# Linear attention and a mixture of four experts on one core: five weight sums change engine, the first batch's small copies are merged, and the start is put in another order

## The chip, the core and the metric

The kernel runs on one core of a Trainium2 chip. The time is device time of one execution in microseconds; a comparison is made between medians of several executions. All times of single instructions below come from one execution that the hardware profiler recorded. The engines are called as in the profile: PE (TensorE), PEld (its weight loads), DVE (VectorE), ACT (ScalarE), POOL (GpSimd) and SP (SyncE, which here only issues DMAs).

## The reference

Two stages follow each other. With `phi(x) = where(x > 0, x, exp(x) - 1) + 1`:

```python
q_p, k_p = phi(q), phi(k)                          # 8 batches, 8 heads, 576 tokens, 64 wide
kv  = einsum('bhsd,bhse->bhde', k_p, v)             # 64 x 64 for each head
z   = sum(k_p, axis=s)
x   = einsum(q_p, kv) / (einsum(q_p, z) + 1e-06)   # 4608 tokens x 512
p   = probs / (probs.sum(-1) + 1e-09)
out = sum over e of p[:, e] * (relu(x @ w1[e]) @ w2[e])   # w1: 512 x 1024, w2: 1024 x 512, 4 experts
```

The kernel computes `phi(x)` as `min(exp(x), max(x + 1, 1))`: one exponential on ACT, one linear part (add, then max) on DVE or POOL, and one minimum on DVE.

## The kernel before, in words

**Tiles.** The 4608 tokens are nine tiles of 512: the first 512 tokens of each of the eight batches, and one tile of all that is left over. A tile passes through the attention of its batch and then through all four experts. Both layers of an expert are done as seven products of quarter blocks in place of eight (a scheme of Strassen's kind). `Block` (L841 to L941) is layer 1, with the products p1, p2, p6, p5, p7, p4, p3 and the sum c22; `layer2_product` (L806) is layer 2, called m in the lists (m12.51 is the fifth product for tile 1, expert 2). The scheme needs sums of weights: `weight_sums` (L758, the steps s0.0 to s3.3, DVE) for w1 and `weight_sums2` (L775, the steps t0.0 to t3.3) for w2. Step t2.1 is part 1 of expert 2. Each is one subtraction of 128x1024 fp16 elements with both inputs in SBUF. Sums of hidden values (L797 to L803, hs) and of tokens (L868, ts) run on POOL. Tile 0 does layer 1 of expert 0 without the scheme, in `layer1_half` (L675, steps L00 to L31, each cut into pieces), and layer 2 of its experts as plain matmuls (y). The sums of w2 are therefore read from tile 1 on alone.

**Batch 0.** Batch 0 has code of its own, the class `First`. Its inputs come in pieces: k and v by pairs of heads (`load_kv`, lk0 to lk3 and lv0 to lv3), q in four pieces of 128x512 (`load_q`, lq0 to lq3). For each piece of k there is an exponential (`k_exp`, L583, ke), a linear part (`k_lin`, L586, kl) and a minimum (`k_min`, L590, km); v is cast (`v_cast`, L593, vc, on the engines of `VC`: pieces 0 and 3 POOL, 1 DVE, 2 ACT). For q the same three are qe (L601), ql (L604) and qm (L607), and then a transposition of four blocks on PE with a copy (`q_turn`, L615, qT). `kv` (L621 to L639) makes kv and z of a pair of heads: 18 matmuls of 64x65 into one PSUM tile, the two heads on different partitions, and then two copies of 64x65 into `kvz`, whose other blocks hold zeros from a memset (L199). `CFG["KC"]` says which engine does each of the eight copies. `x_norm` (L648 to L652, steps nd00 to nd11) multiplies q by `kvz` and normalises; `x_half` (L662, xT) transposes x, after which layer 1 of tile 0 can start. The step nd01 needs pairs 0 and 1, nd11 and nd10 pairs 2 and 3.

**What sets the order.** Every step is a Python generator. The order on every engine is that in which the steps are advanced. For the start of the kernel, up to tile 1, it is the list `CFG["EARLY"]`: a name in it advances that step by one piece, so that a name which stands twice first issues its matmuls and later its copy. What the list does not name is sorted by due positions behind it. The list orders DMAs as well: steps w100 to w231 are 512 KB loads of weights (w1 of expert 1, first half, is w110; w2 of expert 1 is w210 and w211), issued by POOL, and k0 to v3, q0 to q3, rk and rv are later batches' loads on POOL. The first loads of batch 0 are issued by SP and ACT. `warm` (L1016) puts matmuls on PE that only read zeros (`qz`) and compute nothing; `CFG["WARM"]` says how many go with each warm step.

**Engines at the change.** In `QL`, the i-th letter says where the linear part of q's piece i runs: V is DVE, P is POOL. In the list before, the first steps of q are in the order qe0, ql0, ql3, qm0, and pieces 2 and 3 follow behind piece 0's.

Of the kernel before, what the change touches and what calls it, by code (L numbers as in the profile page):

```python
# [11 lines left out]
FP32 = mybir.dt.float32  # L12
FP16 = mybir.dt.float16
AO = mybir.AluOpType
# [22 lines left out]
            kv=34.0,  # L37
# [19 lines left out]
            kv=19.1,  # L57
# [15 lines left out]
            kv=19.1,  # L73
# [21 lines left out]
    "QL": 'VVPV',  # L95
    "QT": 'AAAA',
    "KC": ('AA', 'AV', 'VA', 'AA'),
# [3 lines left out]
    "WARM": (14, 3, 2, 1, 5),  # L101
    "BANK": {'qT0': 'py', 'qT1': 'b', 'nd00': 'py', 'nd00+': 'b', 'kv2': 'py', 'xT00': 'b', 'kv3': 'b', 'nd10+': 'b', 'L00': 'b', 'L10': 'py', 'nd01': 'b', 'xT01': 'py', 'nd11+': 'b', 'L20': 'e', 'L30': 'e', 'L01': 'e', 'L11': 'py', 'L21': 'py', 'L31': 'b', 'b1.qT3': 'py', 'b1.nd30': 'py', 'b1.nd21': 'b', 'b1.q1': 'b', 'b1.qT1': 'py', 'b1.nd01': 'py', 'b1.xT2': 'b', 'b1.nd11': 'py', 'b1.xT0': 'b'},
    "EARLY": (
# [36 lines left out]
def kernel(  # L140
# [10 lines left out]
    nc = tc.nc  # L151
# [6 lines left out]
    P = 128  # L158
    HP = P // 2
# [37 lines left out]
    for i in range(2):  # L197
        kvz = pconst.tile([P, NPAIR, 2, DE], FP16, tag=f"kvz{i}", name=f"kvz{i}")
        nc.vector.memset(kvz, 0.0)  # L199
        kvzs.append(kvz)  # L200
# [26 lines left out]
    def aps(shape, dtype, name, more=""):  # L227
        return ppm.tile(shape, dtype, tag=CFG["BANK"].get(now[0] + more, "s"), bufs=2, name=name)
# [321 lines left out]
    class First(Batch):  # L550
# [70 lines left out]
        def kv(self, i, engs):  # L621
            ps = aps([P, DE], FP32, "psum_kv")
            for t in range(TK):
                for u in range(2):
                    us = slice(u * HP, (u + 1) * HP)
                    nc.tensor.matmul(
                        out=ps[us],
                        lhsT=kpos[us, i, t],
                        rhs=vpos[us, i, t],
                        start=t == 0,  # L630
                        stop=t == TK - 1,
                        skip_group_check=True,
                    )
            for u in range(2):
                yield
                us = slice(u * HP, (u + 1) * HP)
                (engs[u].copy if engs[u] is nc.scalar else engs[u].tensor_copy)(
                    out=self.kvz[us, i, u], in_=ps[us]
                )  # L639
# [135 lines left out]
    def weight_sums2(e, part):  # L775
        if part == 0:
            t2_sb[e] = pw.tile([P, 3, FH, DH], FP16, tag=f"t2_{e}", name=f"t2_{e}")
        w, tw = w2_sb[e], t2_sb[e]
        b11, b12 = w[:, 0:FH, 0:DH], w[:, 0:FH, DH:Dm]
        b21, b22 = w[:, FH:FC, 0:DH], w[:, FH:FC, DH:Dm]  # L780
        if part == 0:
            nc.vector.tensor_tensor(out=tw[:, 0], in0=b12, in1=b11, op=AO.subtract)
        elif part == 1:
            nc.vector.tensor_tensor(out=tw[:, 1], in0=b22, in1=tw[:, 0], op=AO.subtract)
        elif part == 2:
            nc.vector.tensor_tensor(out=tw[:, 2], in0=b21, in1=tw[:, 1], op=AO.subtract)
        else:
            nc.vector.tensor_tensor(out=b12, in0=b22, in1=b12, op=AO.subtract)
# [234 lines left out]
    with tc.manual_schedule(  # L1023
# [7 lines left out]
        def put_at(pos, name, *g):  # L1031
            work.append((pos, len(work), name, g))

        put_at(0, "lpr0", load_probs, nc.sync, True)
        for i in range(4):
# [11 lines left out]
            put_at(0, f"kv{i}", b0.kv, i, [on[y] for y in CFG["KC"][i]])  # L1047
# [122 lines left out]
```

## Time and profile before

| | us |
|---|---|
| median of 3 runs (484.61 to 485.6) | 484.77 |
| the profiled execution | 484.06 |
| its span | 482.3 |
| PE busy | 474.5 |
| DVE, ACT, POOL busy | 377.6, 331.4, 356.1 |
| first real matmul of layer 1 (L675) | 16.10 |
| weights landed: w110, w111, w200, w201 | 20.74, 23.28, 26.39, 29.34 |
| w120, w121, w130, w131 | 33.41, 35.90, 48.30, 51.65 |
| w220, w221, w231, w230 | 55.68, 58.80, 61.31, 63.97 |

The span is that of the profiled execution; 1.8 us of its time lie around it. A row of the timeline has the start, the duration, the engine, the line, the operation with its output and inputs, and the size; "x2" joins neighbouring rows of one line, and the brackets name the idle time ahead and the instruction that ended it. A row of the windows gives the busy time of every engine in a stretch; the number before the last but one is the granted clock of PE, and the next the DMA engines' mean busy share (it can exceed 1).

### The profile page before, as it was taken

How to read it: one execution, taken by the hardware profiler on the slowest of the kernel's cores; microseconds unless marked ns; L12 is line 12 of the kernel's file. 1: busy time of each engine (PE TensorE's matmuls, PEld its weight loads, DVE VectorE, ACT ScalarE, POOL GpSimd, SP SyncE). 2: the span in 40 equal slices, each digit the busy share in tenths (PEclk: the TensorE clock that was granted, in tenths of full speed). 3: DMA queues.
4: the chain of work that ended last, by engine and by line, in shares of the span. 5: the costliest groups of instructions: out<-in, count | busy, mean ns of one | idle time of the engine just before them, and what ended most of it. 6: DMA issues, size and time to landing. Idle time of an engine off the chain costs nothing.

```text
span 482.3 us, 12013 instructions
## 1 busy us (share of the span) xinstructions
PE 474.5 (98%) x4565; PEld 407.4 (84%) x4565; DVE 377.6 (78%) x794; ACT 331.4 (69%) x662; POOL 356.1 (74%) x340
## 2 busy tenths in 40 slices
PE   7999999999999999999999999999999999999997
PEld 3766766898889888998889888988898888888886
DVE  5778988997868895889679885988787756775677
ACT  4689989956895599649874888478954465446540
POOL 5566044789866986789777977697769877987775
PEclk9999999999999999999999999999999999999999
DMA  8999986442445154533552436323230020003002
GB/s 292 219 218 256 232 212 210 124 112 83 135 140 115 39 160 154 119 59 117 173 134 62 112 123 170 78 73 112 65 68 12 2 88 2 0 1 89 2 1 87
DMA packets 80025, 53.67 MB, mean 111 GB/s; under 512 B 45088, under 2 KB 72736, under 8 KB 79968
## 3 DMA queue, kind: packets, MB, share of 16 engines
q1 hardware_dynamic: 69920, 40.56, 30.6%
q0 software_dynamic: 8800, 11.27, 12.1%
q10 hardware_dynamic: 1248, 1.08, 0.7%
q8 instruction: 35, 0.57, 0.5%
q14 instruction: 22, 0.18, 0.1%
HBM read 45.16 MB, written 9.44 MB: 113 GB/s over the span
## 4 chain that ended last, share of the span: by engine, by line
PE 96%; DVE 1%; DMA 1%; issue 0%; ACT 0%; SPq 0%; DVEq 0%
PE py L830 39%; PE pb L887 25%; PE pe L887 19%; PE py L735 6%; PE ph L675 1%; PE psum_nd L492 1%; PE psum_kv L464 1%; DMA rawq<-in_q_dram 1%; PE pb L830 1%; PE pe L830 1%; DVE kpos L586 0%; PE psum_nl L510 0%; PE psum_num L648 0%; PE psum_xh L662 0%; DVE qp L607 0%
## 5 line engine op out<-in xcount | busy, mean ns | idle before, releaser
L726 DVE SCALAR_TENSOR_TENSOR acc<-py,p_sb,acc 128x256 f32<-128x256 f32 (+1 forms) x382 | 182.3, 489 | 42.3 <-PE py L830 38.3
L871 DVE CUSTOM_DVE_ANT_0 h<-pe,u 128x512 f16<-128x512 f32 x140 | 96.2, 689 | 45.5 <-PE pe L887 27.8
L887 PEld LDWEIGHTS <-w 128*128 128x128 f16 x1120 | 108.9, 98 | 16.2
L797 POOL TENSOR_TENSOR hs<-h 128x512 f16<-128x512 f16 x64 | 74.6, 1165 | 56.9 <-DVE h L871 52.8
L830 PEld LDWEIGHTS <-h 128*128 128x128 f16 x1024 | 99.6, 98 | 11.5
L830 PE MATMUL py<-w,h 128*128 128x256 f16 x744 | 106.4, 273 | 0.0
L898 ACT COPY u<-pb 128x512 f32<-128x512 f32 x140 | 82.5, 592 | 29.9 <-PE pb L887 27.8
L799 POOL TENSOR_TENSOR hs<-hs,h 128x512 f16<-128x512 f16 x64 | 73.9, 1155 | 26.3 <-PE py L830 23.8
L887 PEld LDWEIGHTS <-s 128*128 128x128 f16 x840 | 81.2, 98 | 12.0 <-DVE s L767 0.2
L887 PE MATMUL pb<-tt,w 128*128 128x256 f16 x560 | 83.9, 273 | 0.0
L830 PEld LDWEIGHTS <-hs 128*128 128x128 f16 x768 | 74.5, 98 | 8.8 <-issue 0.2
L803 POOL TENSOR_TENSOR hs<-h,hs 128x512 f16<-128x512 f16 x64 | 74.4, 1162 | 0.9 <-PE py L830 0.7
L830 PE MATMUL py<-t,hs 128*128 128x256 f16 x496 | 74.1, 273 | 0.0
L801 POOL TENSOR_TENSOR h<-h 128x512 f16<-128x512 f16 x64 | 73.9, 1154 | 0.1
L920 ACT ACTIVATE h<-pe 128x512 f16<-128x512 f32 x70 | 42.0, 601 | 41.3 <-PE pe L887 40.7
L913 ACT COPY pe<-pb 128x512 f32<-128x512 f32 x70 | 40.0, 572 | 42.0 <-PE pb L887 15.8
L941 ACT ACTIVATE h<-pb 128x512 f16<-128x512 f32 x70 | 41.9, 601 | 6.0 <-PE pb L887 5.9
L887 PE MATMUL pe<-tt,s 128*128 128x256 f16 x280 | 42.0, 273 | 0.0
L887 PE MATMUL pb<-tt,s 128*128 128x256 f16 x280 | 41.8, 273 | 0.0
L887 PE MATMUL pe<-xT,s 128*128 128x256 f16 x248 | 37.1, 273 | 0.0
L887 PE MATMUL pb<-xT,w 128*128 128x256 f16 x248 | 37.1, 273 | 0.0
L830 PE MATMUL py<-w,hs 128*128 128x256 f16 x248 | 37.0, 273 | 0.0
(132 smaller groups left out, 594.4 us busy)
## 6 DMA issues: line engine op xcount, KB each, us to landing
w<-in_moe_w_dram POOLq DMA_DIRECT2D x14, 512.0 KB, 10.6
out_dram<-acc SPq DMA_DIRECT2D x28, 256.0 KB, 2.6
rawb<-in_k_dram SPq DMA_DIRECT2D x24, 256.0 KB, 3.0
rawb<-in_q_dram SPq DMA_DIRECT2D x24, 256.0 KB, 2.7
rawb<-in_v_dram SPq DMA_DIRECT2D x24, 256.0 KB, 2.7
out_dram<-acc SPq DMA_DIRECT2D x12, 128.0 KB, 2.4
w<-in_moe_w_dram POOLq DMA_DIRECT2D x4, 256.0 KB, 5.5
rawb<-in_k_dram POOLq DMA_DIRECT2D x4, 256.0 KB, 10.4
```

Source lines behind the costliest of these rows:

```text
L726: nc.vector.scalar_tensor_tensor(out=acc, in0=ps, scalar=pscal, in1=acc, op0=AO.mult, op1=AO.add)
L797: nc.gpsimd.tensor_tensor(out=hs[0], in0=a21, in1=a22, op=AO.add)
L799: nc.gpsimd.tensor_tensor(out=hs[1], in0=hs[0], in1=a11, op=AO.subtract)
L801: nc.gpsimd.tensor_tensor(out=a21, in0=a11, in1=a21, op=AO.subtract)
L803: nc.gpsimd.tensor_tensor(out=hs[3], in0=a12, in1=hs[1], op=AO.subtract)
L830: nc.tensor.matmul(out=ps, lhsT=lhsT(k), rhs=rhs[:, k], start=first and k == 0, stop=k == FH - 1, skip_group_check=True,)
L871: nc.vector._custom_dve(TENSOR_ADD_SAT, out=out, in0=ps, in1=u, s0=BIG, s1=0.0)
L887: nc.tensor.matmul(out=ps[:, kk], lhsT=lk(kc), rhs=rhs[:, kc], start=first and kk == 0 and kc == 0, stop=kc == 1, skip_group_check=True,)
L898: nc.scalar.copy(u, self.b)
L913: nc.scalar.copy(self.e5, self.b)
L920: nc.scalar.activation(self.h[:, :, 0, 0:NH], self.e5, AF.Relu)
L941: nc.scalar.activation(self.h[:, :, 1, 0:NH], self.b, AF.Relu)
```

## The change

Four things are changed.

- `QL` is VVVV: the linear part of q's piece 2 (128x512) runs on DVE where POOL did it.
- `kv` of batch 0 writes the two heads of a pair into separate columns of a 128x130 PSUM tile. One matmul of zeros (128x130) opens the tile, and one copy of 128x130 on ACT, zeros and all, takes the place of the two of 64x65. The memset of the first `kvz` goes.
- `TP` names five parts of `weight_sums2` (t2.0, t2.1, t2.2, t3.0 and t3.1) that run on POOL; the others stay on DVE.
- `WARM` has 26 matmuls in place of 25, 13 at first and then single ones. `EARLY` is written anew for all engines and reaches a few steps further. In its start the pieces of q stand in the order in which they land: piece 2 and 3 ahead of piece 0. Of the first four weight loads w101 moves up; the loads behind w111 come as rk0, rk1, w200, k2, w201, k1, w120, w121, k0, w210, k3, v0, q1, w211 and so on; the last ones as w220, q3, w221, q2, w230, then t2.0 on the same engine, and w231 behind it.

```diff
-    "QL": 'VVPV',
+    "QL": 'VVVV',
     "QT": 'AAAA',
-    "KC": ('AA', 'AV', 'VA', 'AA'),
+    "TP": {2: (0, 1, 2), 3: (0, 1)},
+    "KC": 'AAAA',
...
-    "WARM": (14, 3, 2, 1, 5),
+    "WARM": (13,) + (1,) * 13,
...
     "EARLY": (
-        "lq2 lq3 lq0 lk0 qe0 ql0 ql3 qm0 kl0 lk1 lpr0 ke0 km0 qe2 ql2 qm2 lv0 ke1 kl1 km1 warm0 qT0 lv1 lk2 qe3 qm3 warm1 qT2 qT0 vc0 w100 warm2 kv0 vc1 qT2",
-        "warm3 kv1 lk3 kv0 kv0 kl2 kv1 kl3 w102 kv1 nd01 lv3 nd01 warm4 xT11 xT01 ke2 km2 qT3 w103 vc3 lv2 ke3 vc2 nd00 w101 km3 xT01 w110 xT11 w111 kv3 k3 kv2",
...
+        "lq2 lq3 warm0 lk0 lq0 qe2 qe3 lk1 ql2 ql3 qe0 qm3 ql0 qm2 qm0 kl0 ke1 ke0 km0 lpr0 lv0 lv1 warm1 warm2 warm3 warm4 warm5 qT0 warm6 lk2 qT2 vc0 lk3",
+        "w100 w102 warm7 warm8 lv3 qT2 qT0 ke2 kl1 vc1 lv2 km1 warm9 kv0 w101 w103 vc3 kv0 ke3 w110 warm10 kl3 km3 kl2 w111 rk0 rk1 w200 k2 w201 k1 w120 w121",
+        "k0 w210 k3 v0 q1 w211 lq1 rv0 v2 rv1 v3 v1 q0 w130 w131 kv1 warm11 kv1 nd01 warm12 nd01 vc2 qe1 warm13 nd00 qT3 xT01 xT11 kv3 xT01 qT3 xT11 ql1 km2",
...
-        nc.vector.memset(kvz, 0.0)
+        if i:
+            nc.vector.memset(kvz, 0.0)
...
-        def kv(self, i, engs):
-            ps = aps([P, DE], FP32, "psum_kv")
+        def kv(self, i, eng):
+            ps = aps([P, 2, DE], FP32, "psum_kv")
+            nc.tensor.matmul(
+                out=ps.rearrange("p u d -> p (u d)"),
+                lhsT=qz[:, 0, 0],
+                rhs=qz.rearrange("p a u c -> p (a u c)")[:, 0 : 2 * DE],
+                start=True,
+                stop=False,
+                skip_group_check=True,
+            )
             for t in range(TK):
                 for u in range(2):
                     us = slice(u * HP, (u + 1) * HP)
                     nc.tensor.matmul(
-                        out=ps[us],
+                        out=ps[us, u],
                         lhsT=kpos[us, i, t],
                         rhs=vpos[us, i, t],
-                        start=t == 0,
+                        start=False,
                         stop=t == TK - 1,
                         skip_group_check=True,
                     )
-            for u in range(2):
-                yield
-                us = slice(u * HP, (u + 1) * HP)
-                (engs[u].copy if engs[u] is nc.scalar else engs[u].tensor_copy)(
-                    out=self.kvz[us, i, u], in_=ps[us]
-                )
+            yield
+            (eng.copy if eng is nc.scalar else eng.tensor_copy)(out=self.kvz[:, i], in_=ps)
...
     def weight_sums2(e, part):
+        eng = nc.gpsimd if part in CFG["TP"].get(e, ()) else nc.vector
...
-            nc.vector.tensor_tensor(out=tw[:, 0], in0=b12, in1=b11, op=AO.subtract)
+            eng.tensor_tensor(out=tw[:, 0], in0=b12, in1=b11, op=AO.subtract)
...
```

The other parts of `weight_sums2` take `eng` in the same way.

More of the change, by code (lines that the diff above doesn't have):

```diff
@@ L781, in weight_sums2 @@
         if part == 0:
-            nc.vector.tensor_tensor(out=tw[:, 0], in0=b12, in1=b11, op=AO.subtract)
+            eng.tensor_tensor(out=tw[:, 0], in0=b12, in1=b11, op=AO.subtract)
         elif part == 1:
-            nc.vector.tensor_tensor(out=tw[:, 1], in0=b22, in1=tw[:, 0], op=AO.subtract)
+            eng.tensor_tensor(out=tw[:, 1], in0=b22, in1=tw[:, 0], op=AO.subtract)
         elif part == 2:
-            nc.vector.tensor_tensor(out=tw[:, 2], in0=b21, in1=tw[:, 1], op=AO.subtract)
+            eng.tensor_tensor(out=tw[:, 2], in0=b21, in1=tw[:, 1], op=AO.subtract)
         else:
-            nc.vector.tensor_tensor(out=b12, in0=b22, in1=b12, op=AO.subtract)
+            eng.tensor_tensor(out=b12, in0=b22, in1=b12, op=AO.subtract)
     def hidden_sum(h, hs, i):
@@ L1046 @@
             put_at(0, f"qT{i}", b0.q_turn, i, on[CFG["QT"][i]])
-            put_at(0, f"kv{i}", b0.kv, i, [on[y] for y in CFG["KC"][i]])
+            put_at(0, f"kv{i}", b0.kv, i, on[CFG["KC"][i]])
             put_at(0, f"nd{i // 2}{i % 2}", b0.x_norm, i // 2, i % 2)
```

58 rows, old and new, of the table nl are left out of this document.

## The prediction

> **What bounds the kernel now.** I read the busy shares first, then the chain that ended last, then the table of windows, and only then single rows of the timeline. The page says that TensorE carries the span:
>
> ```profile
> PE 474.5 (98%) x4565; PEld 407.4 (84%) x4565; DVE 377.6 (78%) x794; ACT 331.4 (69%) x662; POOL 356.1 (74%) x340
> ...
> PE 96%; DVE 1%; DMA 1%; issue 0%; ACT 0%; SPq 0%; DVEq 0%
> ```
>
> The reader is to see that an engine other than PE can matter only where PE has a hole. The windows tell where the holes are (start and end, length, then the busy time of PE, PEld, DVE, ACT and POOL with counts, the granted clock and the DMA share):
>
> ```profile
> 0.00:5.00 5.00, 3.80 (x9) 1.35 (x10) 1.53 (x4) 1.28 (x1) 1.56 (x10) 1.00 0.55 170
> 5.00:10.00 5.00, 3.61 (x25) 1.40 (x25) 3.57 (x8) 3.72 (x7) 3.50 (x4) 1.00 1.06 399
> 10.00:15.00 5.00, 3.73 (x72) 2.45 (x72) 4.24 (x11) 3.04 (x10) 4.98 (x9) 1.00 1.20 256
> 15.00:20.00 5.00, 4.67 (x88) 4.09 (x87) 3.71 (x11) 3.09 (x10) 2.91 (x5) 1.00 1.17 211
> 20.00:25.00 5.00, 5.00 (x50) 4.48 (x48) 3.91 (x9) 3.83 (x9) 1.97 (x3) 1.00 1.17 239
> ```
>
> From 20 us on PE is full, and it stays so to about 479 us. Before that most of its busy time is warm-up matmuls (L1016), which compute nothing. I counted PE's columns: the real matmuls hold 456.5 us at full rate. Of these 3.62 us lie ahead of the first step of layer 1 (L675, 16.10 us), so 12.48 us are lost there; by 22.9 us the loss is 12.60 us, and it grows by only 0.1 us up to 117 us. Some 3 us more are the tail. So the change can win only in the first 16 us, and can lose wherever it opens a hole in the full stretch behind. The DMA share is above 1.0 from 5 to 64 us: weights arrive at a fixed pace, and that is the second bound.
>
> What sets the 16.10 us is the chain of batch 0. Its middle in the timeline (start, duration, engine, line; in brackets the idle time ahead):
>
> ```profile
> 11.04 1.33 DVE L586 TENSOR_SCALAR kpos<-krawt 128x576 f16<-128x576 f32 x2
> 11.18 0.48 PE L626 MATMUL psum_kv<-vpos,kpos 64*64 64x65 f16 x18 [0.49 <-DVE vpos L593]
> ...
> 11.70 0.21 ACT L637 CAST kvz<-psum_kv 64x65 f16<-64x65 f32 x1 [0.86 <-PE psum_kv L626]
> ...
> 12.40 0.23 DVE L637 CAST kvz<-psum_kv 64x65 f16<-64x65 f32 x1
> 12.68 0.22 PE L648 MATMUL psum_num<-kvz,qT 128*128 128x128 f16 x1 [0.77 <-DVE kvz L637]
> ```
>
> The reader is to see that pair 1's sums are ready near 11.7 us, but the second half of their copy stands behind two linear parts on VectorE until 12.40, and PE waits 0.77 us for it.
>
> **Part 1: the first q pieces, VVPV to VVVV and a new order.** Ahead of that middle stand these rows:
>
> ```profile
> 4.33 1.92 POOL L604 TENSOR_SCALAR qp<-rawq 128x512 f16<-128x512 f32 x1 [2.90 <-DMA rawq<-in_q_dram]
> ...
> 6.22 0.76 DVE L604 TENSOR_SCALAR qp<-rawq 128x512 f16<-128x512 f32 x2 [3.71 <-DMA rawq<-in_q_dram]
> 6.22 0.63 ACT L601 ACTIVATE ee<-rawq 128x512 f16<-128x512 f32 x1 [3.06 <-DMA rawq<-in_q_dram]
> ```
>
> Pieces 2 and 3 landed at 4.25 and 4.61 us, but ACT and DVE queue them behind piece 0, which landed at 6.20. The order after puts them first: linear parts at 4.3 and 4.7 (0.42 us, in place of POOL's 1.92), exponentials at 4.3 and 4.8 (0.62), one minimum at 5.5 (0.42). From 6.2 only piece 0 and one minimum are left, so k's linear part starts near 7.25 and pair 0's minimum ends near 8.7. With the same row durations I get kv0 at 8.8 (before 9.89) and kv1 at 10.45 (11.18), which now waits for the second v cast. That is 0.7 us at kv1.
>
> **Part 2: one copy for a pair.** Two 64x65 copies (ACT 0.21, DVE 0.23) become one 128x130 copy on ACT; by the 64x65 row below and the 128x512 copy (0.59) above I take 0.28 us. It no longer stands behind VectorE: pair 1 is copied at about 11.43, the numerators run at 11.5 where the second half ran at 12.68, the normalisation at 12.05 instead of 13.03. PE pays one 128x130 zero matmul a pair, 4 x 0.055 = 0.22 us. The zero memset of one buffer (0.49 us) lies in the idle start of DVE and gains nothing.
>
> From there ql1, km2 and qm1 (DVE), the second normalisation (14.0 to 14.9) and the copy of xT11 follow, and I get the first layer-1 step at **14.45 us** against 16.10. Ahead of it lie 3.62 + 0.22 + 0.09 = 3.93 us of PE work, as the order of PE's steps shows, 0.22 of them the zeros. Loss: 14.45 - 3.71 = 10.74 against 12.60, that is **1.86 us won if nothing is late behind it**.
>
> **What is late next.** Two things. First, weights. Their landing times hardly move, as the first loads keep their order and the queue is full: w110 20.74, w111 23.28, w120 32.5, w131 51.6, w220 54.9, w221 58.1 (those behind w111 shifted by where the new order of POOL's issues puts each, at 2.55 us for 512 KB). Counting 0.108 us for each 256-wide matmul ahead, the first use of each lies 6.06, 8.66, 18.2, 36.64, 39.7 and 42.3 us of PE work behind the first L. A hole opens unless the first L, without holes, would start at 14.68, 14.62, 14.3, 15.0, 15.2 and 15.8. So landings alone take the start back to about 15.0 to 15.8 in effect. Second, small waits that I find by laying the new order over the row durations: nd11 for pair copies 0.15, nd10 for a q copy 0.3, first cuts of the third and fourth L group 0.2, p5.010 behind three ACT operations of batch 1 0.4, batch 1's kv 0.25. They sum to 1.3 us. A PE delayed by one of them is no longer early for the weights, so the two do not add: effective start 14.45 + 1.3 = 15.75, past all landings but the last by 0.05. Gain 1.86 - 1.3 = **0.56, say 0.6 us**.
>
> **Part 3: five sums of layer 2 to POOL.** On DVE a 128x1024 sum takes 0.69 us, 5 x 0.61 start to start = 3.0 us freed between 60 and 115 us. POOL's 128x512 sums take 1.155 us (64 of them), so 1024 take 2.2 us, an estimate, 11 us in all. Their first readers are products of tile 1 after 109 us, and POOL was idle 47 to 64 us, so the duration itself costs nothing: even 3.5 us each would move only the first hidden sums. Freed DVE time is worth nothing where PE is full (below nothing excluded; above, the 0.1 us of drift bounds it). What is not free is this:
>
> ```profile
> 64.36 1.16 POOL L868 TENSOR_TENSOR tt<-xT 128x512 f16<-128x512 f16 x1 [16.89 <-ACT xT L536]
> ...
> 67.65 1.15 POOL L868 TENSOR_TENSOR tt<-xT 128x512 f16<-128x512 f16 x1
> ```
>
> ```profile
> 65.23 0.84 DVE L788 TENSOR_TENSOR w<-w 128x1024 f16<-128x1024 f16 x1
> ...
> 68.44 0.90 DVE L782 TENSOR_TENSOR t<-w 128x1024 f16<-128x1024 f16 x1
> ```
>
> Usual is 0.69. The two sums start while POOL's sum runs and end 0.55 and 0.54 us after POOL's end: as if they got going only when POOL let go, less 0.15. [...]
>
> [...] Bounds 0 and 2.05 us; I take 0 for the forecast, as t2.0 cannot start before w220 has landed (about 55), when s3.0, s3.1 and s3.3 (52 to 53.7 now) are done, and keep the rest as a rival.
>
> WARM goes from 25 to 26 matmuls (0.43 us at first, 0.213 after 5.87 us); they fill waits in PE, and the clock was granted at 1.00 throughout. Single ones between steps may delay a step by up to 0.2 us; this is in the range. [...]
>
> **Sum.** 484.06 (profiled) - 0.6 = 483.46; the median of the runs is 0.71 above the profiled execution, so 484.77 - 0.6 = **484.2**.
>
> **Rivals.**
> - *Full head gain* (0.22). The small waits do not come or lie side by side, and the landings allow a start of 14.7 to 15.0: gain 12.60 - (14.7 to 15.0 - 3.71) = 1.6 to 1.3 us, 483.2 to 483.5. For it: the waits are read from modelled ends of matmuls. Against it: w131, w220 and w221 bind at 15.0 to 15.8.
> - *The change does not do what it says* (0.18). The chain is early but the weights, or the new waits, take all back: loss again 12.4 to 12.8, gain 0.2 to -0.2, 484.6 to 485.0. For it: w200 (slack 0.58 before) and w221 have next to none after. One landing 0.4 us later than I put it takes 0.4.
> - *Blocked sums* (0.15), the slower end. POOL's 2.2 us sums hold s3.2 or t0.2, and with them batch 1's normalisations that PE waits for. One block of 2.05 less 0.3 slack, less the gain of 0.6, is 1.15 us slower, 485.9; it decides from a block of 0.9 us on.
> - *Forecast* (0.45): 0.2 to 1.2 us faster, 483.6 to 484.6.
>
> **How the numbers follow.** 0.2% is 0.97 us, about what a measurement of this kernel can tell from no change. Faster by more: the full gain 0.22 and a third of the forecast, 0.37. Slower by more: most of the blocked sums and a few hundredths of late landings, 0.17. Within: 0.46. The range runs from the full gain with its 1.86 us, 482.9, to one block, 486.0; beyond it lie two blocks, or late landings and a block.
>
> **What would show it.** Right: kv1 near 10.5 and its single copy by 11.5; first L675 row near 14.5; then small PE holes of 0.1 to 0.4 between 15 and 60 us, summing to some 1.3 us, most released by DVE, ACT or weights' DMA; POOL rows of 2.2 us at L787 to L793. Wrong: holes of over 1 us at p6.030 or batch 1's x with a DVE row of 1.5 to 2.7 us in front (blocked); no holes and a first L at 14.5 (full gain); a first L at 16 or later, through a kv1 that still waits for v; or warm-up rows at 0.43 us after 7 us.

## The result, and the profile after

The changed kernel takes 485.75 us (median of 22 runs, 485.44 to 488.06), the kernel before 484.63 us (22 runs, 483.85 to 486.41): a ratio of 1.0026 with a 95% interval of 1.0016 to 1.0036, some 1.3 us slower (1.1 by the two medians), where 0.6 us faster was forecast. The profiled execution of the changed kernel, 486.91 us with a span of 485.1, is one of its longer ones (15 of the 22 have spans of 483.7 to 484.2); its stalls are therefore read here for their causes, and the sizes are taken from the medians and ratios of the experiments.

Page of the kernel after, the busy times and the chain that ended last:

```profile
PE 476.7 (98%) x4570; PEld 408.2 (84%) x4570; DVE 374.9 (77%) x787; ACT 332.4 (69%) x660; POOL 365.5 (75%) x344
...
PE 90%; DVE 3%; ACT 3%; DMA 1%; issue 1%; ACTq 0%
```

Six per cent of the chain have left PE (96% before): two went to DVE (1% before), three to ACT (0% before) and one to issue (0% before); DMA has kept its 1%. The windows of the kernel after (columns as before) say where:

```profile
15.00:20.00 5.00, 4.96 (x61) 4.25 (x59) 3.71 (x10) 2.36 (x8) 2.84 (x4) 1.00 1.16 208
...
25.00:30.00 5.00, 4.67 (x36) 3.34 (x35) 2.81 (x9) 4.47 (x10) 2.60 (x4) 1.00 1.18 240
...
60.00:65.00 5.00, 3.74 (x33) 2.46 (x32) 4.97 (x10) 3.40 (x7) 2.15 (x2) 1.00 0.72 129
```

The last of these stretches in the kernel before:

```profile
60.00:65.00 5.00, 5.00 (x44) 3.25 (x43) 4.89 (x11) 3.14 (x6) 0.64 (x1) 1.00 1.08 198
```

The stretch 15 to 20 is fuller than before (4.96 in place of 4.67), as meant. But PE, which had no hole from 20 us on, now has one of 1.26 us between 60 and 65 and smaller ones at 25 to 30 (0.33), 50 to 55 (0.16) and from 75 to 100 (0.44 in all). Counted by PE's columns as in the prediction, the loss is 11.24 us at the first L (before 12.48 there), 12.55 at 53 us (before 12.46), and in this execution 3 us more by 120 us, where before adds 0.3. Such a count is good to some 0.2 us: the prediction has 12.60 for before at 22.9 us, and a loss cannot shrink; and by the matmul rows that the traces hold, after is still 0.2 us ahead at 53. So the head did win, the win was gone by 53 us as nearly as this can tell, and the slowdown arises behind it.

Timeline of the kernel after, the engines around the largest hole:

```profile
57.90 2.12 POOL L792 TENSOR_TENSOR t<-w,t 128x1024 f16<-128x1024 f16 x1 [0.42 <-DMA w<-in_moe_w_dram]
57.97 2.60 DVE L776 TENSOR_TENSOR s<-w,s 128x1024 f16<-128x1024 f16 x1
60.49 0.67 DVE L375 SCALAR_TENSOR_TENSOR qp<-qp,psum_ee 128x512 f16<-128x512 f16 x1
61.63 0.74 DVE L733 SCALAR_TENSOR_TENSOR acc<-py,p_sb,acc 128x512 f32<-128x512 f32 x1
62.43 0.38 PE L451 MATMUL psum_qT<-identh,qp 128*128 128x128 f16 x4 [1.19 <-DVE acc L733]
```

VectorE's sum s3.2 (L776) starts 0.07 us behind POOL's t2.1 (L792) and takes 2.60 us where its like takes 0.69; it ends 0.55 us behind POOL's end. What stands behind it on VectorE comes some 1.9 us late, and PE stands still for a PSUM tile that the accumulation (L733) has to read first. This is the rival that I had called blocked sums.

And the timeline of the kernel after in the head:

```profile
10.82 0.90 DVE L593 TENSOR_TENSOR kpos<-kexp,kpos 128x576 f16<-128x576 f16 x1 [0.35 <-ACT kexp L586]
11.36 0.88 POOL L596 CAST vpos<-vrawt 128x576 f16<-128x576 f32 x1
11.64 0.91 DVE L589 TENSOR_SCALAR kpos<-krawt 128x576 f16<-128x576 f32 x1
12.48 0.19 DVE L658 RECIPROCAL recip<-psum_den 128x8 f32<-128x8 f32 x1
13.45 0.40 PE L669 MATMUL psum_xh<-identh,x_sb 128*128 128x128 f16 x4 [1.14 <-DVE x_sb L659]
```

Two rows of VectorE around POOL's cast take 0.90 in place of 0.45; PE waits 1.14 us for the normalisation behind them. The first L675 step (now L682) came at 15.05 us: 1.05 earlier than before, 0.6 later than I had put it.

### The profile page after: what moved, and what is told of

It is laid out like the page before. It is cut to its first block, busy times and chain, and to the rows that moved or that the text cites. A ratio compares the mean times of both kernels' runs of the same rounds, so it can differ in the third digit from the quotient of the medians.

```text
span 485.1 us, 12019 instructions
## 1 busy us (share of the span) xinstructions
PE 476.7 (98%) x4570; PEld 408.2 (84%) x4570; DVE 374.9 (77%) x787; ACT 332.4 (69%) x660; POOL 365.5 (75%) x344
## 4 chain that ended last, share of the span: by engine, by line
PE 90%; DVE 3%; ACT 3%; DMA 1%; issue 1%; ACTq 0%
PE py L838 39%; PE pb L895 23%; PE pe L895 18%; PE py L742 3%; PE warm_ps L1024 1%; PE psum_nd L495 1%; PE ph L682 1%; PE psum_kv L467 1%; DMA rawb<-in_k_dram 1%; PE pb L838 1%; DMA out_dram<-acc 1%; ACT pe L921 1%; ACT psum_ee L370 1%; PE pe L838 1%; DVE h L879 1%
## 5 line engine op out<-in xcount | busy, mean ns | idle before, releaser
L733 DVE SCALAR_TENSOR_TENSOR acc<-py,p_sb,acc 128x256 f32<-128x256 f32 (+1 forms) x382 | 182.0, 488 | 44.7 <-PE py L838 38.0
L805 POOL TENSOR_TENSOR hs<-h 128x512 f16<-128x512 f16 x64 | 74.4, 1162 | 53.1 <-DVE h L879 48.7
L807 POOL TENSOR_TENSOR hs<-hs,h 128x512 f16<-128x512 f16 x64 | 74.4, 1162 | 25.2 <-PE py L838 21.5
L838 PEld LDWEIGHTS <-hs 128*128 128x128 f16 x768 | 74.4, 98 | 8.7 <-issue 0.2
L838 PE MATMUL py<-t,hs 128*128 128x256 f16 x496 | 74.4, 273 | 0.0
L895 PE MATMUL pe<-xT,w 128*128 128x256 f16 x248 | 37.2, 273 | 0.0
```

Of the source, the lines that this page charges most:

```text
L733: nc.vector.scalar_tensor_tensor(out=acc, in0=ps, scalar=pscal, in1=acc, op0=AO.mult, op1=AO.add)
L805: nc.gpsimd.tensor_tensor(out=hs[0], in0=a21, in1=a22, op=AO.add)
L807: nc.gpsimd.tensor_tensor(out=hs[1], in0=hs[0], in1=a11, op=AO.subtract)
L838: nc.tensor.matmul(out=ps, lhsT=lhsT(k), rhs=rhs[:, k], start=first and k == 0, stop=k == FH - 1, skip_group_check=True,)
L895: nc.tensor.matmul(out=ps[:, kk], lhsT=lk(kc), rhs=rhs[:, kc], start=first and kk == 0 and kc == 0, stop=kc == 1, skip_group_check=True,)
```

## The experiments

Theory A: where a sum of VectorE and a POOL operation meet, one holds the other until it is through, as the two rows of before suggest (0.84 and 0.90 us in place of 0.69, ended 0.55 and 0.54 us behind POOL's sum); POOL's 2.1 us sums hold s3.2 or t0.2, and batch 1's normalisations behind them. Theory B: the new order of the start loses the time, wherever the sums run. All ratios are to the kernel before on the same chip.

**The sums back on VectorE, in their places.**

```diff
-    "TP": {2: (0, 1, 2), 3: (0, 1)},
+    "TP": {},
```

> The kernel after with its five sums back on VectorE, at the places the list gives them; all else as after. Theory A (POOL's sum blocks s3.2): the row of s3.2 (2.60 us at 57.97 in the trace of after) falls to about 0.7, PE's hole of 1.36 us at 62.4 goes, and the time comes to 484.3 to 484.9, that is, 0.9 to 1.4 us under after. Theory B (the new order of the start and its small waits lose the time, the engine of the sums does not matter): still 485.4 or more. Theory C (VectorE's 3.0 us of relief are worth something): slower than after, 486 or more.

Measured: 491.73 us, ratio 1.0145 (1.0127 to 1.0164). Theory A's and theory B's numbers are missed; theory C's (the relief of VectorE is worth something, 486 or more) is met, but by a wait that it did not name. The hole at 62 is gone, but the list has four of the sums side by side, and on VectorE they run into POOL's token sums. Timeline and then PE's waits of this run:

```profile
66.62 0.68 DVE L790 TENSOR_TENSOR t<-w 128x1024 f16<-128x1024 f16 x1
67.33 1.64 DVE L792 TENSOR_TENSOR t<-w,t 128x1024 f16<-128x1024 f16 x1
68.90 1.63 DVE L790 TENSOR_TENSOR t<-w 128x1024 f16<-128x1024 f16 x1
70.56 1.52 DVE L792 TENSOR_TENSOR t<-w,t 128x1024 f16<-128x1024 f16 x1
```

```profile
PE pb L895 <- ACT pe L921: 4.7, 1, 4.7
```

Three of the four are held, by POOL's sums at 67.3 to 71.5; the ACT copy that releases PE waits 4.73 us for VectorE. So this run tells more of the places of the sums than of their engine. The control that this run does give: s3.2, at its old place (57.79), took 0.68 us without POOL's sum beside it.

**s3.2 alone out of the way.**

```diff
-... b1.nd10 s3.3 y1.03 ...   ... c22.030 s3.2 b1.qm3 ...
+... b1.nd10 s3.3 s3.2 y1.03 ...   ... c22.030 b1.qm3 ...
```

> The kernel after with one step moved: VectorE does s3.2 right behind s3.3 (about 53.7 us), ahead of POOL's first sum, where it stood behind batch 1's first normalisations (57.97). Theory A: s3.2 takes 0.7 us, no hole at 62.4, 484.2 to 484.8. Theory B: 485.4 or more. If the step instead delays batch 1's normalisations by its 0.6 us, a hole of 0.3 to 0.6 near 54 to 56 takes its place and the time is near 485.

Measured: 486.26 us, ratio 1.0027 (1.0017 to 1.0037): no gain, so theory A's time (484.2 to 484.8) is missed and theory B's (485.4 or more) met. Timeline, the two sums of VectorE and POOL's t3.0:

```profile
54.33 0.68 DVE L776 TENSOR_TENSOR s<-w,s 128x1024 f16<-128x1024 f16 x1
61.25 2.12 POOL L790 TENSOR_TENSOR t<-w 128x1024 f16<-128x1024 f16 x1 [0.97 <-DMA w<-in_moe_w_dram]
62.21 1.71 DVE L794 TENSOR_TENSOR t<-w,t 128x1024 f16<-128x1024 f16 x1
```

s3.2 is short again, but VectorE, no longer late, now brings t0.2 just behind the start of POOL's next sum. It ends 0.55 us behind POOL's end, and PE stands still for 0.50 us at 65.1. The hold has moved, so the time does not decide between A and B here.

**POOL's sums in halves.** Each of the five as two of 128x512 (`for c in (slice(0, 2), slice(2, 4))` around the instruction).

> The kernel after with each of POOL's five sums cut into two of 128x512. Theory A as an exclusive hold for one whole instruction: s3.2, if it starts behind POOL, is held by one half only, about 1.1 us less: its row falls from 2.60 to 1.2 to 1.7, the hole from 1.36 to 0 to 0.5, and the time to 484.5 to 485.2. If VectorE were only slowed in proportion while POOL is at work, the row would stay near 2.6 and the time near 485.7. Theory B: 485.4 or more.

Measured: 485.9 us, ratio 1.0019 (1.0010 to 1.0029). Timeline:

```profile
57.83 2.71 POOL L795 TENSOR_TENSOR t<-w,t 128x512 f16<-128x512 f16 x2 [0.27 <-DMA w<-in_moe_w_dram]
57.96 1.57 DVE L776 TENSOR_TENSOR s<-w,s 128x1024 f16<-128x1024 f16 x1
```

Half the instruction, a hold shorter by 1.03 us (2.60 to 1.57); and POOL's pair takes 2.71 where an undisturbed pair takes 2.27, as if its second half had waited for VectorE (s3.2 ends at 59.53, the pair 1.01 us later, at 60.54). By these rows the hold follows the length of POOL's instruction, as theory A says, and is not a slowing in proportion. PE's hole between 60 and 65 fell from 1.26 to 0.41 us. The time missed theory A's 484.5 to 485.2 and hardly fell: in this execution there are 0.77 us of holes between 75 and 80, where after has 0.13, behind a wait of ACT of 1.74 us for the load of batch 2 that comes up again below.

**Part 1 alone, on the kernel before.** VVVV, and the first q pieces as they land.

```diff
-"lq2 lq3 lq0 lk0 qe0 ql0 ql3 qm0 kl0 lk1 lpr0 ke0 km0 qe2 ql2 qm2 lv0 ke1 kl1 km1 warm0 qT0 lv1 lk2 qe3 qm3 warm1
+"lq2 lq3 lq0 lk0 qe2 qe3 ql2 ql3 qe0 qm3 ql0 lk1 lpr0 qm2 qm0 kl0 ke0 km0 lv0 ke1 kl1 km1 warm0 qT0 lv1 lk2 warm1
```

> Before, with part 1 alone: the linear part of q's piece 2 on VectorE, and the first q pieces in the order in which they land; all else as before. My prediction's step: kv0 and kv1 0.7 us earlier or more than in before (9.89 and 11.18); but the copy of pair 1 still stands on VectorE behind two linear parts, so the first L gains only 0.2 to 0.7 and the time 0 to 0.5 (484.1 to 484.7). Rival: weights decide, no change in the time even if L is earlier.

Measured: 484.84 us, ratio 0.9994 (0.9981 to 1.0007). The first L came at 15.5 in place of 16.1, and PE still waited 1.0 us for the pair's copy on VectorE. No change in the time that this can tell.

**Part 2 alone, on the kernel before.** The changed `kv`, its memset and `KC`, the third `kvN` of each pair taken out of the list.

> Before, with part 2 alone: one zero matmul and one copy on ACT for each pair; all else as before. Pair 1 is copied near 11.9 in place of 12.63, its numerators follow at once, the first L comes 0.3 to 0.7 us earlier less 0.22 us of zero matmuls: 484.2 to 484.9. Rival: other steps of VectorE (the normalisation at 13.03) hold it, no change or 0.2 slower.

Measured: 484.37 us, ratio 0.9986 (0.9976 to 0.9995): faster, with the lowest ratio of all runs here (the interval overlaps those of the other runs with an earlier head). Timeline:

```profile
11.84 0.27 ACT L644 CAST kvz<-psum_kv 128x130 f16<-128x130 f32 x1 [0.96 <-PE psum_kv L635]
...
12.15 0.22 PE L653 MATMUL psum_num<-kvz,qT 128*128 128x128 f16 x1
```

Pair 1's numerators start at 12.15 instead of 12.68, the first L at 15.6. The copy took 0.27 us; 0.28 was estimated.

**Parts 1 and 2 on the kernel before.**

> Before with parts 1 and 2 together, the sums and the order behind the start as before. Part 2 alone gave 0.57 less (ratio 0.9986), part 1 alone 0.1 less (0.9994). If they add: 484.0 to 484.4 where before is 484.8; if the weights hold the rest, no better than part 2 alone (0.5 to 0.6 under before). If the dense part behind them is put out of step, no gain.

Measured: 484.54 us, ratio 0.9991 (0.9982 to 1.0001). The first L is at 14.8, earlier still, and nothing more is won. PE's waits of this run show what came in its place:

```profile
PE ph L680 <- DMA w<-in_moe_w_dram: 0.7, 1, 0.7
PE pb L892 <- DVE s L772: 0.5, 1, 0.5
```

PE waits 0.70 us for weights at 18.7, and 0.5 us for a weight sum (L772) that itself came late because the sum ahead of it on VectorE waited 1.04 us for weights until 52.2. Before has neither wait. Part 2 alone has the second one too (0.5 us), so it is the 0.70 that sets this run apart from it.

**Part 3 alone, on the kernel before.** `TP` and `eng`, with the list as it was.

> Before, with part 3 alone: the five sums on POOL, at the places of before's list, where they come between the token sums of tile 1 (64 to 85 us). Theory A (an exclusive hold, not the order of the start): POOL's 2.1 us sums now lie beside VectorE's other sums t3.x and t2.3, rows there of up to 2.6 us appear, and the token sums of tile 1, which layer 1 of tile 1 reads, come up to 4 us later: 0.5 to 2.5 us slower. Theory B (moving the sums is harmless): within 0.3 of before.

Measured: 490.38 us, ratio 1.0106 (1.0090 to 1.0121), 5.4 us slower, more than twice the worst I had given. PE's waits of this run:

```profile
PE py L832 <- POOL hs L805: 2.3, 1, 2.3
...
PE pb L889 <- POOL tt L870: 1.7, 1, 1.7
```

Here the price is not a hold but POOL's own queue: token and hidden sums that PE reads stand behind sums of 2.1 us. Part 3 needs a list that gives POOL's sums a place of their own, as the list of after does at 54 to 63 us.

**The kernel after again.**

> The kernel after, unchanged, beside the others of this call. In most of its executions (15 of 22) the span was 483.7 to 484.2, in the profiled one 485.1. Theory A: s3.2 and POOL's t2.1 start within 0.1 us of each other, and the one that starts first holds the other; in an execution with a span near 483.8 the row of s3.2 is 0.7 us long and PE has no hole at 62.4, while t0.2, which comes after it, may still be held (1.6 us). Theory B: such an execution has the long row too, and is shorter elsewhere.

Measured: 486.56 us, ratio 1.0036 (1.0023 to 1.0050). The profiled execution was again a long one (span 485.9): POOL's t2.1 started at 57.85, and PE has a hole of 1.2 us. Timeline:

```profile
58.13 2.39 DVE L776 TENSOR_TENSOR s<-w,s 128x1024 f16<-128x1024 f16 x1
```

There is no trace of a short execution of the unchanged kernel, so whether s3.2 goes free in those is not shown. The kernel before, which has no such meeting, spreads as widely (483.85 to 486.41 in its 22 runs).

**Both sums out of the way.**

```diff
-... s3.3 y1.03 ... c22.030 s3.2 b1.qm3 ... b1.xT0 t0.2 p3.030 ... c22.031 y2.13 ...
+... s3.3 s3.2 y1.03 ... c22.030 b1.qm3 ... b1.xT0 p3.030 ... c22.031 t0.2 y2.13 ...
```

> The kernel after with both of VectorE's sums out of the way of POOL's: s3.2 right behind s3.3, and t0.2 behind the last normalisation of batch 1 (near 67). With s3.2 alone moved, t0.2 took 1.71 us at 62.21 beside POOL's t3.0 and PE lost 0.71 us at 65.12. Theory A: that hole goes too, 0.6 to 0.8 under the run with s3.2 alone moved (486.26), 485.4 to 485.7; what then remains over before (0.6 to 0.9) is not the sums. Theory B: no change, 486.2.

Measured: 485.23 us, ratio 1.0008 (0.9998 to 1.0017). Timeline of the two sums:

```profile
54.30 0.68 DVE L776 TENSOR_TENSOR s<-w,s 128x1024 f16<-128x1024 f16 x1
66.33 0.68 DVE L794 TENSOR_TENSOR t<-w,t 128x1024 f16<-128x1024 f16 x1
```

Neither is held, and between 55 and 75 us PE has no hole. Against 1.0036 for the unchanged kernel beside it, two steps in another place take off 1.3 us, though POOL does the same five sums; with s3.2 alone moved, and t0.2 held in its stead, nothing was gained. This is theory A; theory B had no change.

**Part 3 undone in the kernel after, the sums spread.** t2.0 in front of b2.k1, t3.0 behind p6.101, t3.1 behind c22.100, t2.1 behind y3.22, w231 right behind w230.

> The kernel after with part 3 undone: the five sums on VectorE, spread over places like those of before's list (t2.0 near 67, t3.0, t3.1 and t2.1 between 74 and 82), w231 issued right behind w230; the rest of the order as after. Theory A (POOL's sums are the whole loss): 484.0 to 484.7. Theory B (the new order behind 50 us loses by itself): 485.3 or more. Between them: both.

Measured: 487.48 us, ratio 1.0065 (1.0043 to 1.0088): a miss. s3.2 at its old place ran free again:

```profile
57.90 0.68 DVE L776 TENSOR_TENSOR s<-w,s 128x1024 f16<-128x1024 f16 x1
```

but PE then lost time from 77 us on: 1.17 us of holes from 75 to 85, where the run with both cleared has 0.41. Two of the four moved sums stand on VectorE at 75.9 and 77.1, and two of those holes wait for VectorE behind them. The four took 0.68 us each, so it is not that they were held. Against the unchanged kernel beside it (486.56 us, 1.0036) this order is 0.9 us slower by the medians, though the two intervals overlap: with these places the relief of VectorE may be worth more than the holds cost, and I had put it at nothing.

**s3.2 one place up.**

```diff
-... c22.030 s3.2 b1.qm3 ...
+... s3.2 c22.030 b1.qm3 ...
```

and t0.2 as in the run with both cleared.

> As the run with both sums cleared, but s3.2 is moved by one place only: ahead of the saturating sum of c22.030 in front of it, so that it starts near 57.4, still beside POOL's t2.1 (57.85 to 58.2). Theory A as an exclusive hold by whoever starts first: s3.2 takes 0.7, POOL's t2.1 starts or ends some 0.2 to 0.5 later, no hole at 62.4, and the time is that of the run with both cleared (485.2, within 0.4). If any overlap of the two engines slows VectorE: s3.2 takes over 1.2 and the time is 485.8 or more.

Measured: 485.84 us, ratio 1.0029 (1.0019 to 1.0039): the time was missed, the row not. Timeline:

```profile
57.35 0.68 DVE L776 TENSOR_TENSOR s<-w,s 128x1024 f16<-128x1024 f16 x1
57.91 2.12 POOL L792 TENSOR_TENSOR t<-w,t 128x1024 f16<-128x1024 f16 x1 [0.43 <-DMA w<-in_moe_w_dram]
...
74.47 0.63 ACT L367 ACTIVATE kp<-rawb 128x512 f16<-128x512 f32 x1 [1.56 <-DMA rawb<-in_k_dram]
...
79.44 0.60 PE L895 MATMUL pb<-xT,w 128*128 128x256 f16 x4 [0.67 <-ACT h L949]
```

VectorE came first and was all but through when POOL began (0.12 us of overlap), so the two did not contend and the run does not test who goes first; there is no hole at 62. What is lost instead stands at 76 to 80 us, 1.0 us of holes and 1.5 by the count of columns: ACT waits 1.56 us for the last k piece of batch 2, and layer 1 of tile 1 queues behind it. The list of after asks for that load early: it was issued at 69.8, landed at 74.4, and ACT stood in front of it from 72.9; before issues it at 72.7, it lands at 75.2, and ACT reads it at 76.9. In the trace of after, with the hole at 62 ahead of it, the same wait was 0.69 us.

**That load later in ACT's order; t3.2 earlier; the cast off POOL.** Three moves, each on the run with both cleared.

```diff
-... p2.100 b2.k3 ... b1.qTl p7.100 y3.21 ... c22.100 b2.km3 b2.v1 p6.101 ...
+... p2.100 ... b1.qTl p7.100 b2.k3 y3.21 ... c22.100 b2.v1 p6.101 b2.km3 ...
```

> As the run with both sums cleared, and ACT takes batch 2's last k piece (b2.k3) behind the copy of p7.100 in place of ahead of it. In the traces ACT stands 0.6 to 1.7 us still at 73 to 75 us for that piece's load (issued 69.8 to 71.5, landed 73.7 to 75.2; before issued it at 72.7, it landed at 75.2 and ACT read it at 76.9), and the copy and the next products of layer 1 stand behind it; in the run with s3.2 moved by one place PE lost 1.5 us there (76 to 80). Theory D (the new order asks for this load before it has landed): the wait of ACT goes, PE's holes between 75 and 80 go, 0.2 to 0.6 under the run with both cleared (485.23 where before was 484.97). If ACT has slack there: no change.

Measured: 485.09 us, ratio 1.0006 (0.9996 to 1.0016), and all 12 runs within 484.8 to 485.47, where the run with both cleared spread over 484.93 to 486.4. ACT's wait is gone from the trace, PE's holes between 75 and 80 fell from 0.41 to 0.12 us. In the median this is no more than 0.1 us; the spread is smaller, though the two were not run beside each other.

```diff
-... pr1 t2.3 b2.load10 ... c22.101 t3.2 y3.10 ...
+... pr1 t2.3 t3.2 b2.load10 ... c22.101 y3.10 ...
```

> As the run with both sums cleared, and t3.2, which took 1.61 us at 80.44 beside POOL's hidden sums, put ahead of them, right behind t2.3 (near 78.4). Theory A for the rest too: the hold of 0.9 us goes; with it part of PE's holes between 80 and 92 us (1.2 us in that run's trace), 0.2 to 0.6 under 485.2. If these holes come from other waits (ACT behind a load of batch 2 or a store), no change: 485.1 to 485.4.

Measured: 484.79 us, ratio 1.0003 (0.9993 to 1.0014). t3.2 took 0.68 in place of 1.61; the next sum was held in its place (1.28 at 82.66). The interval overlaps that of the run with both cleared.

```diff
-    "VC": 'PVAP',
+    "VC": 'PVAA',
```

with vc3 behind vc2 in the list.

> As the run with both sums cleared, and the cast of v's piece 3 (POOL, 11.4 to 12.3) put on ACT behind piece 2's. In the trace of after k's linear part of piece 2 (L589, 11.64) took 0.91 beside that cast in place of 0.45, and the first normalisation, for which PE waits 1.1 us, came behind it. Theory: the row falls to 0.45, the first normalisation comes 0.3 to 0.45 earlier, and the first L with it; the time falls by up to 0.45, to 484.8 to 485.2, if the small waits and the weights let it through; if they take it back, no change.

Measured: 485.48 us, ratio 1.0016 (1.0006 to 1.0026): the first L came at 14.6, the rows of L593 and L589 fell to 0.46 and 0.45, and the time did not fall.

**The moves together**, on the run with both cleared: t3.2 and the cast, then the load too.

First without the load's move:

> All of these moves together: both sums cleared, t3.2 ahead of the hidden sums, the cast on ACT. If each gives what its theory says, 484.2 to 484.9, at or under before (484.9); if neither gives anything, 485.2.

Measured: 484.76 us, ratio 1.0004 (0.9994 to 1.0015).

Then with it:

> All moves that took a wait away: both sums cleared, t3.2 ahead of the hidden sums, v's last cast on ACT, b2.k3 behind the copy of p7.100. The run without the last move was at 1.0004 of before. If theory D holds, 0.2 to 0.6 less: 0.9990 to 1.0000 of before, 483.9 to 484.4 where before is 484.4; if the remaining loss is elsewhere (weights w130 and w131 hold s3.0 and batch 1's normalisations behind it), 1.0004 again.

Measured: 484.85 us, ratio 0.9995 (0.9983 to 1.0006). Timeline:

```profile
52.35 0.69 DVE L772 TENSOR_TENSOR s<-w 128x1024 f16<-128x1024 f16 x1 [0.61 <-DMA w<-in_moe_w_dram]
```

With the first L at 14.3, VectorE stands 0.61 us for w130 and w131, and PE 0.28 us at 56.24 for a normalisation behind it.

And with s3.2 in the place that it has in the run one place up:

> As the run with all moves, but s3.2 stands only one place ahead of where after has it (near 57.4, before POOL's t2.1 starts) and no longer in front of batch 1's first normalisations. With s3.2 early these come 0.6 us later, and in the traces with the early head PE lost 0.4 to 0.55 us at 56 us to them. If that is the price of s3.2's early place: 0.2 to 0.5 under the run with all moves. If s3.2 then meets POOL's t2.1 after all (POOL starting first), a row of over 2 us and 0.5 to 1.3 over it.

Measured: 484.8 us, ratio 0.9995 (0.9983 to 1.0007): no hold, and no price of the early place of s3.2 that shows in the time. The trace still has ACT wait 1.1 us for batch 2's k, and PE 0.84 us at 78.6, so moving the one load did not take that wait away for good. Neither of the two is clearly faster than before; part 2 alone is.

## Why the prediction was wrong, step by step

- **What bounds the kernel** was right: PE has no slack behind 20 us, and the change could win in the head alone and lose wherever it opens a hole. It did both.
- **Part 1 and part 2** were right in kind, and the size was off. kv1 started at 10.15 (10.45 forecast), the pair was copied by 10.95 (11.43 forecast); but the normalisation came at 12.48, not 12.05, behind two rows of VectorE of 0.90 us that I had put at 0.45. With the cast off POOL they take 0.46 and 0.45, and the first L comes at 14.56, 0.49 us earlier. The prediction shows a row of before that has the same: at 11.04 two linear parts take 1.33 us where two of 0.45 would take 0.90, the first of them 0.73 beside POOL's cast of 10.78 to 11.44. I had read it without asking why. The head's 1.86 us measured 1.36 (at the first L itself, where before has lost 12.48 and not 12.60, 1.74 was forecast and 1.24 came).
- **The small waits** were put at 1.3 us; by 53 us the count gives 1.45 relative to before. The trace has several of those that I had named: matmuls of 256 columns usually start 0.11 us apart, and they stand 0.29 and 0.30 apart at 16.7 and 17.4 (first cuts), 0.60 at 26.5 (behind ACT) and 0.43 at 53.0 (batch 1). Head less waits is thus -0.1 (0.2 by the rows of the trace) and not +0.56. That weights cap any gain of the head is suggested by three runs (both parts on before, the cast, all moves): each brought the first L to 14.3 to 14.8 and then had PE or VectorE wait 0.3 to 1.0 us for weights, with no gain in time over the run without the earlier head. It is not shown: no run moves a load of weights alone, and part 2 alone, the one clear gain, has such a wait as well (1.00 us of VectorE). More than the 0.6 us of part 2 alone was not to be had from the head in any run.
- **Part 3 is the step that failed**: "I take 0 for the forecast", because t2.0 could not start before 55 us, when three of the s sums are done. It started at 54.62 and hit nothing; but t2.1 follows at 57.9, and s3.2, the fourth, stands within 0.1 us of it. The bound I gave, 2.05 us, is nearly what happened (2.60 - 0.69 = 1.91), and the rival's price, 485.9, is within 0.2 us of the time. That the price came so close is partly luck: it is one block of 1.75 less a gain of 0.6, and the runs show 0.9 to 1.4 for the holds, no gain and some 0.3 from elsewhere (below). The rival deserved far more than 0.15: with POOL at work for 6.4 of the 8.5 us from 54.6 and VectorE's two sums due in them, a free passage was the less likely case. The rows show how long VectorE's sum took: 2.60 behind a whole sum of POOL, 1.57 behind half of one, 0.68 at the same place without one. That the first one goes first fits them too, but not a row of the head (last section). No run shows the 0.3 us of slack that the rival's price takes off; in the trace of after, 1.91 us of hold left PE a hole of 1.26 us.
- **"Freed DVE time is worth nothing"** is in doubt too: with the sums back and spread, the order of after was 0.9 us slower than the unchanged kernel beside it (1.0065 and 1.0036 of before, intervals that overlap). How much of that is the full VectorE and how much the places that I chose is open.
- **Not foreseen**: the new order has ACT wait for a load of batch 2. The run with s3.2 one place up shows it where the hold had hidden it. What it costs by itself is open: moving the load took off no more than 0.1 us in the run made for it.

The sum: 1.36 won, 1.45 lost by 53 us, 0.9 to 1.4 by held sums (1.0026 and 1.0036 down to 1.0008 when both are cleared), and some 0.3 left, to which the load of batch 2, t3.2 and the store of an accumulator contribute in the traces. How these last split is open, and so is why the unchanged kernel's executions fall into shorter and longer ones; s3.2 and t2.1 starting within 0.1 to 0.3 us of each other is a candidate, argued and not shown. Of the 1.9 us between the forecast and the result, the held sums, put at nothing, are thus the larger part and the head, put 0.5 too high, the next; without the holds the kernel would still not have been faster.

## What to carry to other kernels

Before work is moved from VectorE to GpSimd, list the operations of VectorE that fall into GpSimd's new busy stretch, and price them at a wait for the GpSimd instruction beside them: here s3.2, with both inputs in SBUF, took 2.60 us in place of 0.68 beside a sum of 2.12 us, and 1.57 beside halves of one. Two rows that read PSUM kept their length beside the next sum in the trace of after (60.95 to 63.07): L733, 0.74 us at 61.63, and L409, 0.41 at 62.29; with part 3 undone and POOL idle there they took 0.75 and 0.41. Moving the two steps that met one was worth 1.3 us; cutting the long ones shortened the hold, but not clearly the time. An instruction order that hangs on which of two engines starts first by 0.1 us is to be priced at the bad outcome. And a head made earlier is worth only what the waits behind it leave: look for the next landing and the next full engine before counting the gain.

## What the runs showed of the hardware

A cast by POOL from fp32 held a VectorE operation with a single SBUF input as well: L589, 0.91 us beside a cast of 0.88 us and 0.45 us with the cast on ACT. L593 ahead of it took 0.90 us at 10.82, though it began 0.54 us before the cast, and 0.46 with the cast on ACT. And in the run with both sums cleared L589 began at 11.33, 0.30 us before POOL's cast (11.63 to 12.32), and took 1.31 us, to 0.32 us behind the cast's end. So by the starts that the profile shows, the one that begins first is not always the one that goes free; why is open. The other direction is seen too: POOL's pair of halves took 0.44 us longer around s3.2 (2.71 against 2.27 us). POOL's 128x1024 subtraction took 2.12 us undisturbed; 2.2 was estimated from the 512-wide row.

In the run with part 3 alone PE waited 2.3 and 1.7 us at a time, and its granted clock was 1.00 in every stretch up to 120 us. The run with the sums back on VectorE, where PE waited 4.7 us at once, has a mean granted clock of 0.993 to 0.996 in its four executions; before, without such a wait, has 0.996 to 1.0, so these means do not tell what the wait did.
